# Eight-step rows for the first four chunks of k and b in a chunked recurrence with a feed-forward block, under a new written-out order

## The chip, the cores and the metric

The kernel runs on one core of a Trainium2 chip. The metric is device time in microseconds; several executions are timed and the median is given. A profile is one more execution, with the time of every instruction and DMA packet. Work is spread over five instruction queues: PE (matrix multiplies and transposes, results in PSUM), DVE and ACT (elementwise work, both can read PSUM), POOL (elementwise work, SBUF only) and SP (issues DMAs).

## The reference

`r, k, v, w, a, b` have the shape (4 batches, 8 heads, 768 steps, 40 features). For each of the 32 heads a 40 x 40 state is carried over the steps; the output of the recurrence goes through a feed-forward block with a squared ReLU:

```python
for t in range(S):
    y[:, :, t] = np.einsum('bhd,bhde->bhe', rt, state)
    Sa = np.einsum('bhde,bhe->bhd', state, at)
    state_decay = state * wt[:, :, None, :] - np.einsum('bhd,bhe->bhde', Sa, bt)
    state = state_decay + np.einsum('bhd,bhe->bhde', vt, kt)
...
h = x @ w_in            # x: (3072, 320), w_in: (320, 2048)
r = np.maximum(h, 0.0)
return (r * r) @ w_out  # w_out: (2048, 320)
```

## The kernel before

The 768 steps are cut into 12 chunks of 64. Inside a chunk the recurrence is written as matrix products; between chunks only the state is carried. The program is a list of named operations (`plan.add`, `ew`, `pe`), and a string `ORDER` (lines 87 to 214) says in which order they are issued and on which engine each one runs: `POOL castA 0` is the operation castA of chunk 0 on POOL; `PE2 TK 0` is the transposition TK of chunk 0, with its result in the second of four PSUM slots (`pb0` to `pb3`). Each engine takes its own operations strictly in that order and waits at the first whose inputs are not there or whose slot is not free. The order was not made at run time; it stands in the source.

What a chunk c does, by the names in `ORDER`:

- Loads on SP, two DMAs each (`load`, line 391): `ldw`, `ldk`, `ldb`, `ldv` in rows of 40 numbers (160 B, one step of one head), token-major, that is with the step on the partition; `lda`, `ldr` in rows of eight steps (1,280 B), with the head pair and the group of eight steps on the partition. Every raw buffer is there twice (`raw_kb` holds k and b of a chunk together). A DMA's semaphore is used again eight DMAs later, so SP issues a DMA only after the one eight before it has landed.
- Decay: `ln` (ACT) takes the logarithm of w into `lnW`; `hi` and `lo` split it into two bf16 parts; PE sums over the steps, once token-major in two halves (`ci h0`, `ci h1`) and once feature-major, with the step along the free axis (`cf`). ACT makes exponentials of these: `ex` (into `Gin`, for the output) and `ei` (with the sign reversed, into `iG`) from ci, `ef` (into `GT`) from cf.
- Keys: `mulKB h0`, `h1` multiply raw k and b by `iG` into `KB` (token-major, bf16); `TK` is 32 transposes of KB on PE, and `tK` copies them out of PSUM to `KBT` (feature-major). KB itself is an operand of `S` and `Y`, KBT of `EN`.
- a and r: `castA`, `castR` convert to bf16 in the order that the transposes want, `TA`, `TR` are 16 transposes each, `tA` multiplies by GT on the way out of PSUM, `tR` copies. Both go to `AR`.
- Recurrence: `EN` (KBT times a; `mEN` masks it), `AS` (a times the state, from chunk 1 on), `EV`, `u0`, `NU`, `u1` (solves for the chunk's right-hand sides in `VU`), `SC` and `S` (new state), `s` (decays it into `STb`), `TS` and `tS` (its transposition, `Sb`).
- Output: `TV`, `tV`, `CX`, `mCX`, `RS`, `Y`, `y`, `yd`, then `XT`, `xt` (x transposed).
- Feed-forward: for four blocks u, `F` (256 input features) and `FL` (the last 64), `f` (ReLU out of PSUM), `q` (square), `O`, then `o` and the store `st`.

The weights come in pieces: `lwl`, `lwi u0` to `u3` (staged in the second buffer of G) with casts `cwl`, `cwi`; `lwo x0` to `x7`, staged in the two `osb` buffers, with casts `cwo`. They share SP's queue with the loads of the chunks.

The lines the change and the prediction touch: 404 to 411 (loads of k and b), 475 to 478 (`ei`), 501 to 509 (`mulKB`), 522 to 534 (`TK`, `tK`), 547 to 556 (`steps`, `turned`, `tA`, which turn a transposed row-of-eight tile), 561 to 562 (what EN reads), and `ORDER`. In the profile all matmuls have line 384, all transposes 388, and copies 365 (DVE), 370 (ACT) and 374 (POOL).

Of the kernel before, what the change touches and what calls it, by code (L numbers as in the profile page):

```python
# [84 lines left out]
HALVES = ()  # L85
O_AFTER = 0
ORDER = """SP ldw 0; SP lda 0; SP ldb 0; SP ldk 0; ACT ln 0; SP ldw 1; POOL hi 0; POOL castA 0; DVE lo 0; PE0
TA 0; SP lda 1; PE1 ci 0 h0; PE2 ci 0 h1; ACT ex 0 h0 g1; PE3 cf 0; ACT ex 0 h1 g0; ACT ei 0 h1;
ACT ex 0 h1 g1; ACT ei 0 h0; SP ldv 0; ACT ef 0; DVE mulKB 0 h1; SP ldw 2; ACT ex 0 h0 g0; DVE
mulKB 0 h0; DVE tA 0 g0; PE2 TK 0; DVE tK 0; ACT ln 1; SP ldk 1; POOL hi 1; DVE tA 0 g1; PE3 EN 0  # L90
g0; POOL lo 1; DVE mEN 0 g0; PE1 EN 0 g1; DVE mEN 0 g1; SP ldb 1; PE2 ci 1 h1; POOL castV 0 g0;
ACT ei 1 h1; POOL castV 0 g1; ACT ex 1 h1 g1; ACT ex 1 h1 g0; POOL castA 1; PE0 EV 0; SP ldr 1;
PE3 cf 1; ACT u0 0; PE1 ci 1 h0; ACT ln 2; PE NU 0; ACT ex 1 h0 g1; PE2 TA 1; POOL hi 2; ACT ef 1;
SP lda 2; DVE lo 2; ACT u1 0 g0; DVE tA 1 g0; ACT ei 1 h0; SP ldv 1; PE3 S 0 g0; DVE tA 1 g1; ACT
ex 1 h0 g0; ACT u1 0 g1; PE1 ci 2 h0; SP ldr 0; ACT ex 2 h0 g1; PE S 0 g1; DVE mulKB 1 h0; PE2 TV
0; DVE mulKB 1 h1; ACT ei 2 h0; DVE s 0 q1; ACT tV 0; SP ldw 3; PE0 TK 1; DVE s 0 q0; SP ldk 2;
DVE tK 1; PE3 TS 0; ACT tS 0; PE2 EN 1 g1; PE0 cf 2; DVE mEN 1 g1; SP ldb 2; PE3 EN 1 g0; ACT ef
2; POOL castR 0; DVE mEN 1 g0; ACT ex 2 h0 g0; POOL castV 1 g1; ACT castA 2; PE2 TR 0; PE0 ci 2
h1; POOL castV 1 g0; ACT tR 0 g0; PE1 AS 1; SP lwl 0; ACT tR 0 g1; POOL castR 1; PE EV 1; ACT ln
3; PE3 CX 0 g0; PE2 CX 0 g1; ACT u0 1; POOL hi 3; DVE mCX 0 g0; ACT ex 2 h1 g1; PE NU 1; POOL lo  # L100
3; ACT ex 2 h1 g0; SP lwi 0 u0; ACT ei 2 h1; DVE mCX 0 g1; PE3 TR 1; ACT u1 1 g0; PE0 TA 2; ACT tR
1 g1; DVE tA 2 g1; PE2 Y 0; SP ldv 2; ACT tR 1 g0; ACT u1 1 g1; PE3 SC 1; DVE mulKB 2 h1; PE1 TV
1; SP ldr 2; PE S 1 g0; DVE tA 2 g0; ACT tV 1; PE S 1 g1; DVE y 0; DVE mulKB 2 h0; ACT cwl 0; DVE
yd 0; PE0 TK 2; DVE s 1 q0; PE1 ci 3 h1; POOL cwi 0 u0; SP lwi 0 u1; PE2 CX 1 g0; DVE tK 2; ACT ei
3 h1; ACT ex 3 h1 g0; ACT ex 3 h1 g1; SP lwo 0 x1; DVE s 1 q1; PE0 cf 3; PE1 EN 2 g0; DVE mCX 1
g0; ACT ef 3; PE3 TS 1; POOL castV 2 g1; SP lwo 0 x0; ACT tS 1; DVE mEN 2 g0; PE0 EN 2 g1; POOL
castR 2; PE2 AS 2; SP ldb 3; POOL castV 2 g0; DVE mEN 2 g1; PE3 ci 3 h0; PE1 XT 0; ACT ex 3 h0 g0;
POOL cwi 0 u1; ACT ei 3 h0; DVE xt 0; PE EV 2; ACT ex 3 h0 g1; SP lwi 0 u3; PE0 CX 1 g1; ACT u0 2;
PE1 FL 0 u1; DVE mCX 1 g1; PE NU 2; SP lda 3; PE3 RS 1; ACT u1 2 g0; PE0 SC 2; PE Y 1; DVE u1 2
g1; SP ldk 3; PE F 0 u1; DVE y 1; SP lwi 0 u2; DVE yd 1; PE S 2 g0; ACT f 0 u1; PE S 2 g1; PE2 TR  # L110
2; DVE s 2 q0; PE3 FL 0 u3; ACT tR 2 g1; POOL cwi 0 u3; DVE s 2 q1; ACT tR 2 g0; SP ldw 4; DVE q 0
u1; POOL castA 3; PE F 0 u3; POOL cwo 0 x0; PE1 TV 2; ACT f 0 u3; DVE cwo 0 x1; PE2 XT 1; PE0 TS
2; SP lwo 0 x2; ACT tV 2; PE3 F 0 u0; DVE tS 2; POOL mulKB 3 h0; DVE xt 1; PE0 TA 3; PE FL 0 u0;
SP lwo 0 x3; DVE tA 3 g1; PE2 FL 1 u3; ACT f 0 u0; PE1 CX 2 g0; POOL cwi 0 u2; DVE tA 3 g0; PE F 1
u3; SP ldv 3; DVE mulKB 3 h1; PE3 F 1 u2; ACT f 1 u3; DVE mCX 2 g0; SP ldr 3; PE0 TK 3; ACT ln 4;
PE FL 1 u2; PE2 FL 1 u1; DVE tK 3; PE1 CX 2 g1; ACT f 1 u2; POOL hi 4; PE F 1 u1; POOL cwo 0 x2;
DVE mCX 2 g1; PE3 F 1 u0; POOL lo 4; ACT cwo 0 x3; PE0 EN 3 g0; ACT f 1 u1; SP lwo 0 x5; PE FL 1
u0; DVE mEN 3 g0; PE1 F 0 u2; ACT f 1 u0; SP lwo 0 x4; PE FL 0 u2; DVE q 0 u0; PE2 EN 3 g1; POOL
castV 3 g0; PE0 cf 4; ACT f 0 u2; DVE mEN 3 g1; PE3 ci 4 h0; SP ldw 5; POOL castV 3 g1; ACT ef 4;
PE1 RS 2; DVE q 0 u2; PE Y 2; ACT ei 4 h0; PE2 AS 3; DVE yd 2; PE EV 3; DVE cwo 0 x5; ACT ex 4 h0  # L120
g1; DVE y 2; PE0 O 0 u0; SP lwo 0 x7; ACT u0 3; POOL cwo 0 x4; DVE q 1 u0; ACT ex 4 h0 g0; POOL
castR 3; ACT q 0 u3; PE1 ci 4 h1; SP lwo 0 x6; PE NU 3; ACT ex 4 h1 g1; PE3 TR 3; ACT u1 3 g0; SP
ldk 4; PE O 0 u1; DVE tR 3 g1; ACT ex 4 h1 g0; DVE u1 3 g1; ACT ei 4 h1; PE O 0 u2; POOL cwo 0 x7;
SP ldb 4; ACT tR 3 g0; ACT ln 5; PE1 XT 2; DVE cwo 0 x6; PE2 TV 3; SP lda 4; POOL hi 5; DVE xt 2;
PE3 SC 3; ACT tV 3; PE S 3 g0; POOL lo 5; PE S 3 g1; PE O 0 u3; DVE s 3 q1; SP ldv 4; DVE s 3 q0;
POOL q 1 u1; PE1 ci 5 h0; ACT o 0; PE2 CX 3 g0; SP ldk 5; PE3 cf 5; ACT ex 5 h0 g0; DVE mCX 3 g0;
PE0 FL 2 u1; ACT ef 5; PE F 2 u1; DVE mulKB 4 h0; ACT ex 5 h0 g1; PE2 F 2 u2; ACT f 2 u1; SP ldb
5; DVE mulKB 4 h1; POOL castA 4; PE3 FL 2 u3; PE FL 2 u2; ACT ei 5 h0; DVE q 2 u1; PE0 TK 4; ACT f
2 u2; PE1 TA 4; PE F 2 u3; DVE tA 4 g0; SP ldw 6; DVE tK 4; PE2 F 2 u0; POOL castV 4 g0; ACT f 2
u3; POOL castV 4 g1; PE FL 2 u0; DVE tA 4 g1; PE0 ci 5 h1; POOL q 2 u3; ACT f 2 u0; PE3 CX 3 g1;  # L130
PE1 O 1 u0; SP lda 5; DVE mCX 3 g1; ACT ex 5 h1 g1; ACT q 2 u0; PE2 EN 4 g1; PE3 EN 4 g0; POOL q 1
u2; DVE mEN 4 g1; PE O 1 u1; ACT ex 5 h1 g0; ACT ei 5 h1; SP st 0; DVE mEN 4 g0; PE0 RS 3; PE Y 3;
POOL mulKB 5 h0; SP ldr 4; PE2 AS 4; DVE y 3; PE EV 4; DVE q 1 u3; PE O 1 u2; SP ldw 7; DVE yd 3;
ACT ln 6; DVE mulKB 5 h1; PE O 1 u3; ACT u0 4; POOL hi 6; POOL q 2 u2; PE NU 4; ACT o 1; PE3 XT 3;
ACT u1 4 g0; PE0 TS 3; SP st 1; DVE xt 3; PE1 TK 5; ACT tS 3; DVE u1 4 g1; PE3 FL 3 u3; POOL castA
5; PE F 3 u3; SP ldv 5; DVE tK 5; POOL castR 4; PE2 TA 5; ACT f 3 u3; POOL lo 6; PE0 TV 4; SP lda
6; DVE tA 5 g1; PE1 O 2 u0; DVE tA 5 g0; DVE tV 4; ACT ln 7; PE3 SC 4; PE S 4 g0; SP ldb 6; PE S 4
g1; PE2 ci 6 h0; DVE s 4 q0; PE0 TR 4; ACT ex 6 h0 g0; PE O 2 u1; SP ldk 6; ACT ei 6 h0; DVE s 4
q1; ACT ex 6 h0 g1; DVE tR 4 g1; ACT tR 4 g0; PE3 cf 6; PE2 EN 5 g0; ACT ef 6; POOL castV 5 g1; PE
O 2 u2; DVE mEN 5 g0; SP ldr 5; POOL castV 5 g0; ACT q 3 u3; PE0 CX 4 g0; PE3 ci 6 h1; DVE mCX 4  # L140
g0; PE2 CX 4 g1; ACT ei 6 h1; POOL hi 7; PE O 2 u3; ACT castA 6; POOL lo 7; DVE mCX 4 g1; PE0 F 3
u0; ACT ex 6 h1 g0; ACT o 2; ACT ex 6 h1 g1; PE FL 3 u0; SP st 2; PE2 EN 5 g1; PE1 TA 6; ACT f 3
u0; DVE mEN 5 g1; PE3 RS 4; PE Y 4; SP ldw 8; ACT q 3 u0; PE0 AS 5; POOL mulKB 6 h1; DVE yd 4; PE
EV 5; DVE tA 6 g1; PE2 FL 3 u1; DVE y 4; SP ldv 7; ACT u0 5; PE F 3 u1; POOL mulKB 6 h0; DVE tA 6
g0; PE3 F 3 u2; SP ldv 6; ACT f 3 u1; PE FL 3 u2; POOL castR 5; PE1 XT 4; PE2 TK 6; ACT f 3 u2;
DVE xt 4; POOL q 3 u1; PE NU 5; DVE tK 6; SP ldr 6; PE1 TR 5; ACT u1 5 g0; PE3 F 4 u0; DVE tR 5
g1; ACT tR 5 g0; ACT u1 5 g1; PE FL 4 u0; PE2 EN 6 g1; PE1 EN 6 g0; ACT f 4 u0; DVE mEN 6 g1; PE0
SC 5; SP lda 7; PE S 5 g0; PE S 5 g1; ACT q 3 u2; PE3 ci 7 h0; DVE s 5 q1; PE2 O 3 u0; SP ldk 7;
ACT ei 7 h0; DVE mEN 6 g0; ACT ex 7 h0 g1; PE O 3 u1; ACT ex 7 h0 g0; SP st0 0; DVE s 5 q0; POOL
castV 6 g0; PE3 TV 5; PE1 ci 7 h1; DVE tV 5; POOL castR 6; PE0 TS 4; ACT ex 7 h1 g1; SP ldb 7; PE  # L150
O 3 u2; ACT ei 7 h1; POOL castA 7; DVE tS 4; ACT ex 7 h1 g0; ACT ln 8; SP ldr 7; PE3 CX 5 g0; PE1
# [66 lines left out]
def kernel(  # L218
# [128 lines left out]
    def evac(name, make, n, reads, writes, free):  # L347

        kind = " ".join(x for i, x in enumerate(name.split()) if i != 1)
        if kind not in HALVES:  # L350
            ew(name, make(slice(0, 2), 2 * n), reads=reads, writes=writes, free=free)
            return
# [607 lines left out]
```

## Time and profile before

| | |
|---|---|
| median of 3 runs | 252.59 us |
| the three runs | 251.22, 252.59, 256.84 us |
| span of the profiled execution | 249.1 us |
| PE, DVE, ACT, POOL busy | 219.2, 183.3, 172.4, 119.3 us |
| DMA packets | 115,179, of them 101,302 under 512 B |
| ACT `iG`<-pb (ei), 24 of them | 0.696 us each |
| ACT `GT`<-pb (ef), 12 | 1.022 us each |
| DVE `KB`<-raw_kb,iG (mulKB), 16; POOL, 8 | 0.992; 1.584 us each |
| DVE `KBT`<-pb (tK), 11 | 1.220 us each |
| DVE `AR`<-pb,GT (tA), 24 | 0.683 us each |
| DVE `Sb`<-pb (tS), 8; ACT, 3 | 0.820; 1.237 us each |
| POOL casts of raw a, r, v to bf16; ACT of raw a | 0.716 to 0.809; 0.736 us each |

The times hold no figure of their own for the profiled execution; the span, from its first to its last instruction, stands in its place. The table of groups gives, per line, engine, tiles and shape, the busy time and the mean of one instruction, so a step of the order is found by the tiles that it writes and reads. "Idle before" is the time that the engine stood still just before such an instruction, with what it waited for. A matmul's duration is that of one instruction from start to end; they overlap, so the distance from start to start is the price of one more.

### The profile page before, as it was taken

How to read it: one execution, taken by the hardware profiler on the slowest of the kernel's cores; microseconds unless marked ns; L12 is line 12 of the kernel's file. 1: busy time of each engine (PE TensorE's matmuls, PEld its weight loads, DVE VectorE, ACT ScalarE, POOL GpSimd, SP SyncE). 2: the span in 40 equal slices, each digit the busy share in tenths (PEclk: the TensorE clock that was granted, in tenths of full speed). 3: DMA queues.
4: the chain of work that ended last, by engine and by line, in shares of the span. 5: the costliest groups of instructions: out<-in, count | busy, mean ns of one | idle time of the engine just before them, and what ended most of it. 6: DMA issues, size and time to landing. Idle time of an engine off the chain costs nothing.

```text
span 249.1 us, 12580 instructions
## 1 busy us (share of the span) xinstructions
PE 219.2 (88%) x5752; PEld 171.4 (69%) x5752; DVE 183.3 (74%) x227; ACT 172.4 (69%) x231; POOL 119.3 (48%) x119
## 2 busy tenths in 40 slices
PE   0458868859997999999999999999999999999991
...
DMA  6999899989998986978868978965580020201121
GB/s 130 168 157 212 158 190 182 229 195 218 224 195 161 157 199 122 189 159 147 184 171 136 179 121 217 157 163 115 119 144 4 4 58 4 56 3 30 26 52 55
DMA packets 115179, 33.58 MB, mean 135 GB/s; under 512 B 101302, under 2 KB 115126, under 8 KB 115126
## 3 DMA queue, kind: packets, MB, share of 16 engines
q1 hardware_dynamic: 114982, 32.62, 65.3%
q8 instruction: 45, 0.74, 1.2%
...
## 4 chain that ended last, share of the span: by engine, by line
PE 51%; SPq 21%; DMA 8%; DVE 6%; ACT 6%; issue 4%; POOL 3%; POOLq 0%; ACTq 0%
PE pb L384 45%; SPq L407 8%; PE pb L388 5%; SPq L431 3%; SPq L421 3%; SPq L400 2%; SPq L882 2%; SPq L414 2%; DMA osb<-in_moe_w_out_dram 2%; DMA G<-in_moe_w_in_dram 2%; DMA raw_w<-in_w_dram 2%; DMA raw_r<-in_r_dram 2%; DVE AR L365 1%; ACT AR L370 1%; DMA out_dram<-osb 1%
## 5 line engine op out<-in xcount | busy, mean ns | idle before, releaser
L384 PE MATMUL pb<-WOUT,G 128*128 128x320 bf16 x384 | 57.2, 300 | 1.1 <-DVE WOUT L365 1.1
L802 ACT ACTIVATE G<-pb 128x1024 bf16<-128x1024 f32 x44 | 44.6, 1021 | 19.3 <-PE pb L384 18.4
L810 POOL TENSOR_TENSOR G<-G 128x1024 bf16<-128x1024 bf16 x21 | 40.8, 1956 | 24.2 <-ACT G L802 24.1
L384 PE MATMUL pb<-XT,WIN 128*128 128x256 bf16 x384 | 48.4, 273 | 2.8 <-POOL WIN L374 2.8
L384 PEld LDWEIGHTS <-G 128*128 128x128 bf16 x384 | 35.3, 98 | 15.8 <-issue 2.3
L384 PEld LDWEIGHTS <-WIN 128*128 128x128 bf16 x384 | 34.9, 98 | 10.4 <-POOL WIN L374 3.3
L578 DVE TENSOR_TENSOR CX<-pb,MSKI 128x1024 bf16<-128x1024 f32 x24 | 29.0, 1220 | 7.4 <-PE pb L384 7.3
L578 DVE TENSOR_TENSOR EN<-pb,MSK 128x1024 bf16<-128x1024 f32 x24 | 29.0, 1221 | 6.5 <-PE pb L384 6.2
L481 ACT ACTIVATE Gin<-pb 64x320 f32<-64x320 f32 x48 | 20.6, 429 | 9.8 <-PE pb L384 9.2
L374 POOL CAST VU<-raw_v 64x640 bf16<-64x640 f32 x24 | 18.7, 777 | 11.8 <-DMA raw_v<-in_v_dram 11.1
L370 ACT ACTIVATE osb<-pb 128x640 f32<-128x640 f32 (+1 forms) x13 | 8.3, 640 | 18.6 <-PE pb L384 18.1
L670 DVE TENSOR_TENSOR STb<-pb,GT 64x640 bf16<-64x640 f32 x22 | 18.0, 820 | 2.9 <-PE pb L384 2.6
L374 POOL CAST hi<-lnW 128x640 bf16<-128x640 f32 x12 | 9.0, 747 | 22.7 <-ACT lnW L453 19.4
L380 DVE TENSOR_TENSOR KB<-raw_kb,iG 128x640 bf16<-128x640 f32 x16 | 15.6, 992 | 5.7 <-DMA raw_kb<-in_b_dram 3.2
L384 PEld LDWEIGHTS <-EN 64*64 64x64 bf16 x768 | 15.3, 114 | 5.9 <-issue 2.7
L475 ACT ACTIVATE iG<-pb 128x640 f32<-128x640 f32 x24 | 16.7, 696 | 3.4 <-PE pb L384 3.2
L553 DVE TENSOR_TENSOR AR<-pb,GT 128x512 bf16<-128x512 bf16 x24 | 15.8, 683 | 2.3 <-PE pb L388 2.0
L384 PE MATMUL pb<-XT,WLAST 64*128 64x256 bf16 x192 | 17.4, 274 | 0.1
L808 DVE TENSOR_TENSOR G<-G 128x1024 bf16<-128x1024 bf16 x13 | 10.4, 805 | 8.6 <-ACT G L802 8.5
L370 ACT ACTIVATE VUT<-pb 128x2048 bf16<-128x2048 bf16 x8 | 15.0, 1874 | 2.2 <-PE pb L388 2.2
L370 ACT ACTIVATE VU<-pb 64x640 bf16<-64x640 f32 x19 | 13.2, 696 | 3.7 <-PE pb L384 3.5
L378 POOL TENSOR_TENSOR KB<-raw_kb,iG 128x640 bf16<-128x640 f32 x8 | 12.6, 1584 | 6.2 <-ACT iG L475 4.5
...
## 6 DMA issues: line engine op xcount, KB each, us to landing
...
```

The lines of the kernel that those rows point to most:

```text
L370: alts.append(("ACT", c_act(n), lambda: nc.scalar.activation(out=o_(), in_=i_(), func=ACTF.Copy, scale=1.0 if scale is None else scale)))
L374: lambda: nc.gpsimd.tensor_copy(out=o_(), in_=i_())))
L380: ("DVE", c_dve(n), lambda: nc.vector.tensor_tensor(out=o_(), in0=a_(), in1=b_(), op=op))]
L384: return lambda: nc.tensor.matmul(out=o_(), lhsT=l_(), rhs=r_(), start=start, stop=stop, skip_group_check=True)
L407: nc.sync.dma_start(out=raw_kb[c % NKBR][rows(g if nm == "b" else 1 - g), NJ * g:NJ * g + NJ, :], in_=half(x, g))
L475: ew(f"ei {c} h{jh}", [("ACT", c_act(2 * n), lambda hb=hb, jh=jh: nc.scalar.activation(out=iG[0][:].rearrange("p (g j) e -> p g (j e)", g= ...
L481: nc.scalar.activation(out=Gin[c % NGI][rows(g), NP * jh:NP * jh + NP, :].rearrange("p j e -> p (j e)"), in_=slot(hb, FP32)[rows(g), g, 0: ...
L553: ew(f"tA {c} g{g}", [("DVE", c_dve(512), lambda g=g: nc.vector.tensor_tensor(out=steps(AR[q2][:, 0, g]), in0=turned(ha, g), in1=steps(GT[ ...
L578: evac(f"m{nm} {c} g{g}", lambda s, n: [("DVE", c_dve(n), lambda: nc.vector.tensor_tensor(out=dst[q2][:, g, s].rearrange("p q i t -> p (q ...
L670: ew(f"s {c} q{q}", [("DVE", c_dve(2 * n), lambda q=q: nc.vector.tensor_tensor(out=STb[q2][rows(q), :, q, 0:D], in0=slot(hs, FP32)[rows(q) ...
L802: ("ACT", c_act(1024), lambda gb=gb, hf=hf: nc.scalar.activation(out=gb, in_=slot(hf, FP32)[:], func=ACTF.Relu)),
L810: ("POOL", 1900, lambda gv=gv: nc.gpsimd.tensor_tensor(out=gv, in0=gv, in1=gv, op=ALU.mult)),
```

## The change

For the chunks in `BY8 = (0, 1, 2, 3)`, k and b are loaded as a and r are, in rows of eight steps, `raw_kb` holding k in its first 16 head places and b in the other 16. They are converted to bf16 (`castk`, `castb`, on POOL or ACT), transposed (`Tk`, `Tb`, 16 transposes each) and multiplied by the reversed-sign exponential of the feature-major sums (`eg`, from cf, in place of the two `ei`) on the way out of PSUM into KBT (`tk`, `tb`, two halves each, on DVE). The token-major KB is then made from KBT by a second transposition (`TU`, 32 transposes) and a copy (`tU`, DVE or ACT). Chunks 4 to 11 go on as before (`keys`). EN reads KBT by halves. The order is another one from the first entry to the last: 1,052 entries instead of 1,032. Entries of the planner's past in the source (`LAT`, `HALVES`, `evac` and so on) are gone; they issued nothing of their own.

```diff
+BY8 = (0, 1, 2, 3)
...
         for nm, x in (("k", k), ("b", b)):
             def go(nm=nm, x=x):
+                if c in BY8:
+                    xv = x[:, :, t0, :].rearrange("b (p q) (k i) e -> q (b p) k (i e)", q=2, i=8)
+                    to = raw_kb[c % NKBR][:].rearrange("p (x q j) e -> p x q (j e)", x=2, q=2)
+                    for q in range(2):
+                        nc.sync.dma_start(out=to[:, int(nm == "b"), q, :], in_=xv[q])
+                    return
...
+    def keys_by8(c, hf):
+        q2 = c % 2
+        igt = iG[0][:].rearrange("p h e -> p (h e)")[:, 0:1024].rearrange(
+            "p (m t) -> p m t", t=L)
+        ew(f"eg {c}", [("ACT", c_act(1024), lambda: nc.scalar.activation(
+            out=igt.rearrange("p (g m) t -> p g m t", g=2),
+            in_=slot(hf, FP32)[:].rearrange("p g (m t) -> p g m t", t=L), func=ACTF.Exp,
+            scale=-1.0))],
+           reads=[hf], writes=[("iG", 0), ("iG", 1)], free=[hf])
+        kb = KB[c % NK]
+        for x, nm in enumerate("kb"):
+            ew(f"cast{nm} {c}", copy_alts(
+                lambda x=x: kb[:, 16 * x:16 * x + 16, 0:D].rearrange(
+                    "p (i q) e -> p q i e", q=2),
+                lambda x=x: raw_kb[c % NKBR][:, 16 * x:16 * x + 16, :].rearrange(
+                    "p (q i) e -> p q i e", q=2), 640, engines=("POOL", "ACT")),
+               reads=[("raw", nm, c % NKBR)], writes=[("KB", c % NK, x)])
+            h = ("A", "T" + nm, c)
...
+            pe(f"T{nm} {c}", "R", 64, ms, reads=[("KB", c % NK, x)], writes=[h], alloc=[h])
+            for g in range(2):
+                ew(f"t{nm} {c} g{g}", [("DVE", c_dve(512), lambda g=g, x=x, h=h:
+                                        nc.vector.tensor_tensor(
+                    out=steps(KBT[q2][:, NP * g:NP * g + NP, g if x else 1 - g]),
+                    in0=turned(h, g), in1=steps(igt[:, NP * g:NP * g + NP]), op=ALU.mult))],
+                   reads=[h, ("iG", 0), ("iG", 1)], writes=[("KBT", q2, x, g)], free=[h])
...
+        pe(f"TU {c}", "R", 64, ms, reads=KX, writes=[h2], alloc=[h2])
+        ew(f"tU {c}", copy_alts(
+            lambda: kb[:].rearrange("p (i q) e -> p q i e", q=2)[:, :, :, 0:D],
+            lambda: slot(h2, BF16)[:].rearrange("p q (i e) -> p q i e", e=64)[:, :, :, 0:D],
+            1280, True),
+           reads=[h2], writes=[("KB", c % NK, 0), ("KB", c % NK, 1)], free=[h2])
...
+            if c not in BY8:
...
+        if c in BY8:
+            keys_by8(c, hf)
+        else:
+            keys(c)
```

The new order around chunk 2, cut to a few entries:

```
PE1 AS 1; ...; ACT ef 2; ACT ex 2 h1 g1; ACT ex 2 h1 g0; PE3 TA 2; ...; PE2 Tk 2; ACT eg 2;
DVE tA 2 g0; PE0 ci 2 h0; ACT castR 1; ACT castb 2; DVE tA 2 g1; ...; PE EV 1; PE3 Tb 2; ...; ACT u0 1
```

On SP the weights' pieces `lwo x6`, `lwo x7` now stand ahead of `lda 4`, `ldk 4`, `ldb 4`, `ldw 6`, `ldv 4`; in the order before `lwo x7`, `lwo x6` stood ahead of `ldk 4`, `ldb 4`, `lda 4`, `ldv 4`.

More of the change, by code (lines that the diff above doesn't have):

```diff
@@ L82, in issue @@
         assert len(done) == len(self.ops)
[L85 to L151, printed above, removed]
@@ new lines @@
+h0; PE1 O 0 u0; PE NU 3; PE O 0 u1; POOL q 1 u1; PE2 XT 2; DVE q 0 u2; ACT ex 4 h1 g0; PE0 TR 3;
+DVE xt 2; ACT u1 3 g0; SP lda 4; ACT u1 3 g1; PE3 TV 3; SP ldk 4; PE2 SC 3; PE S 3 g0; DVE tR 3 g1;
+ACT tR 3 g0; POOL q 0 u3; SP ldb 4; POOL q 1 u0; ACT tV 3; PE S 3 g1; POOL castA 4; DVE s 3 q0; PE
+O 0 u2; PE3 CX 3 g0; DVE s 3 q1; POOL q 1 u2; POOL mulKB 4 h1; PE0 CX 3 g1; DVE mCX 3 g0; PE2 FL 2
+u1; PE F 2 u1; ACT cwo 0 x6; DVE mCX 3 g1; PE3 F 2 u2; ACT cwo 0 x7; PE O 0 u3; PE0 F 2 u0; PE FL 2
@@ new lines @@
+u0; ACT ln 5; SP ldw 6; SP ldv 4; ACT f 2 u1; DVE o 0; PE FL 2 u2; ACT f 2 u2; PE2 FL 2 u3; DVE hi
+5; POOL castV 4 g0; PE1 TA 4; PE F 2 u3; SP ldr 4; DVE lo 5; PE3 O 1 u0; ACT f 2 u0; PE O 1 u1; ACT
+f 2 u3; SP ldb 5; ACT q 2 u3; DVE tA 4 g0; DVE mulKB 4 h0; DVE tA 4 g1; POOL q 2 u1; PE2 ci 5 h0;
+SP ldk 5; ACT ei 5 h0; ACT ex 5 h0 g1; SP lda 5; PE1 TK 4; PE0 cf 5; POOL castR 4; PE O 1 u2; ACT
+ef 5; PE0 ci 5 h1; DVE q 1 u3; POOL q 2 u2; SP st 0; DVE tK 4; SP lda 6; PE1 EN 4 g0; SP ldk 6;
+POOL mulKB 5 h0; DVE mEN 4 g0; SP ldv 5; ACT ex 5 h0 g0; ACT ln 6; ACT ex 5 h1 g1; ACT castV 4 g1;
@@ new lines @@
+g0; DVE s 6 q1; PE0 EN 7 g1; DVE s 6 q0; ACT ei 8 h1; POOL q 4 u2; DVE mEN 7 g1; ACT ex 8 h1 g1;
+PE1 cf 8; PE2 RS 6; ACT f 5 u0; ACT ef 8; PE Y 6; PE3 AS 7; PE EV 7; SP lda 9; PE1 TR 8; DVE y 6;
+PE0 TA 8; DVE yd 6; ACT u0 7; SP ldk 9; ACT tR 8 g0; DVE tR 8 g1; SP ldr 10; POOL castR 7; DVE tA 8
+g1; DVE tA 8 g0; PE2 ci 8 h0; SP ldb 8; POOL castV 8 g0; PE NU 7; ACT q 5 u1; ACT ei 8 h0; PE1 O 4
+u0; ACT ex 8 h0 g1; PE O 4 u1; ACT ex 8 h0 g0; PE O 4 u2; DVE mulKB 8 h1; ACT ln 9; POOL hi 9; POOL
+castA 9; SP st 3; POOL q 5 u0; DVE u1 7 g0; PE O 4 u3; ACT u1 7 g1; DVE mulKB 8 h0; POOL castV 8
```

300 lines of the change are left out of this document (176 added, 124 removed).

## The prediction, made before the changed kernel had run

> **What bounds the kernel now.** First the page: the span and the engines in forty slices.
>
> ```profile
> span 249.1 us, 12580 instructions
> PE 219.2 (88%) x5752; PEld 171.4 (69%) x5752; DVE 183.3 (74%) x227; ACT 172.4 (69%) x231; POOL 119.3 (48%) x119
> ...
> PE   0458868859997999999999999999999999999991
> ...
> DMA  6999899989998986978868978965580020201121
> ```
>
> No engine is full overall, but PE is from slice 10 (62 us) on, and DMA is full before it. The busy table over stretches that I cut at the chunk recurrence puts figures on this (PE, PEld, DVE, ACT, POOL busy, clock, DMA share, GB/s):
>
> ```profile
> 10.00:30.00 20.00, 14.00 (x400) 11.29 (x396) 13.91 (x16) 14.62 (x23) 6.32 (x9) 1.00 1.02 180
> 30.00:60.00 30.00, 22.80 (x770) 18.40 (x766) 22.65 (x28) 21.86 (x32) 11.74 (x13) 0.89 0.92 198
> 60.00:76.40 16.40, 15.99 (x414) 12.36 (x414) 12.37 (x16) 14.45 (x21) 9.12 (x11) 1.00 0.92 204
> 76.40:244.00 167.60, 164.47 (x4154) 127.92 (x4150) 126.57 (x146) 118.25 (x154) 88.20 (x71) 1.00 0.56 113
> ```
>
> From 76.4 us PE is 98% busy, so loads are worth something before that only. Third, PE's timeline, for the dates: `STb,AR` is AS, the state going into chunks 1, 2 and 3; `VU,EN` is EV; the first `XT,WIN` lines are F 0; `VU,KB` at 76.35 is S 3.
>
> ```profile
> 31.37 0.48 PE L384 MATMUL pb<-STb,AR 128*64 128x80 bf16 x16
> 31.78 0.68 PE L384 MATMUL pb<-VU,EN 64*64 64x40 bf16 x32
> ...
> 44.54 0.48 PE L384 MATMUL pb<-STb,AR 128*64 128x80 bf16 x16
> ...
> 50.98 1.05 PE L384 MATMUL pb<-XT,WIN 128*128 128x256 bf16 x8
> ...
> 56.04 1.05 PE L384 MATMUL pb<-XT,WIN 128*128 128x256 bf16 x8 [2.84 <-POOL WIN L374]
> ...
> 69.15 0.48 PE L384 MATMUL pb<-STb,AR 128*64 128x80 bf16 x16
> ...
> 76.35 0.66 PE L384 MATMUL pb<-VU,KB 128*64 128x40 bf16 x32
> ```
>
> The 2.84 us is the one long wait of PE that a late weight load causes. I compare three stages: to AS 2 (44.54), to S 3 (76.35), to PE's end (244.0).
>
> **Loads.** Eight (k and b of chunks 0 to 3) go from 2,048 rows of 160 B to 256 rows of 1,280 B. The price of the second kind, from a window that holds one 320 KB store in such rows:
>
> ```profile
> q1 hardware_dynamic: 288, 0.33, 13.7%
> ```
>
> 13.7% of 10 us = 1.37 us. The whole run: 65.3% of 249.1 = 162.7 us; its 13,824 larger packets at 1.37/256 take 74.0; the other 88.7 us over 48 loads are 1.85 each. Gain 8 x 0.48 = 3.8 us. The trace's packet records (means of 16.0 and 75.7 ns, over 16 engines) give 2.05 and 1.21, and SP needs two issues of some 0.65 us for a load, so 1.3: 8 x 0.75 = 6.0 us. Ends 3.8 and 6.0; I take 6.0, since mixed loads are what the records hold. Up to the last WOUT piece 18 loads in short rows at 2.05, 8 in long rows at 1.3 and weights of 19.1 (2,560 packets at 58.7 ns, 2,048 at 75.7) make 66.4 us; now 10 and 16: 60.4. [...]
>
> **Work of chunks 0 to 3.** ACT: eight `iG` exponentials at 0.70 (5.6) become four at 1.02 (the GT row) with five casts at 0.74 and two tU at 1.24 (the Sb row): 10.3, +4.7. DVE: seven mulKB at 0.99 and four tK at 1.22 (11.8) become sixteen multiplies out of PSUM at 0.683 (AR<-pb,GT, the same shapes; 0.82, the STb row, as upper end) and two tU at 0.82: 12.6, +0.8 (to +3.0). POOL: one mulKB (1.58) becomes three casts (2.25). PE: 128 more 64x64 transposes; sixteen take 0.61 us at 21.77 us and 0.41 at 30.34, that is 27 and 15 ns each: 1.9 to 3.4. All this stands in the stretch where PE, DVE and ACT are 70 to 76% busy: room is there, but not on the chain.
>
> **Stage 1, to AS 2.** I follow the new order by hand with these durations. In before's timeline a load lands 7.2 to 9.2 us after the sum of the loads up to and with it (raw_r of chunk 2: 37.8, landed 44.95; the last WIN piece: 50.9, landed 60.06); I use 7.5, and 9 for weights. Chunk 0: cf 0 ends 9.7, eg 10.8, ef 11.9; DVE tb, tA, tk to 15.9; mEN 0 to 18.3, tU 0 19.2, EV 0 19.4 (before: 19.3), s 0 done 25.7 (before 26.9). EN of chunk 0 no longer waits for the token-major form. Then two waits are new. v 1 stands at 23.3 us of loads, as before, so EV 1 cannot be early. And EV 1 now stands in PE's queue behind ci 2 h0, whose slot eg 2 must free: on ACT ef 2 ends 31.5, two exponentials 32.5, eg 2 33.5, so EV 1 comes at 34.0, 2.2 later than 31.78, and on ACT u0 1 behind castR 1 and castb 2 at 35.7; behind these wait NU, u1, S of chunk 1. What follows is quicker, since k 2, b 2 and v 2 are long there (v 2 stood at 36.5 us of loads, now at 30): u1 38.7, S 1 40.5; DVE, after mEN 2 g1, ends s 1 at 42.9; AS 2 at 43.1. Stage 1: -1.4. SP's wait for castb 0 (raw_kb is reused by ldb 2, ahead of ldk 1 and lda 1) is hidden by four loads in flight; uncovered, 0.74.
>
> **Stage 2, to S 3.** F 0 u1 comes at 52.5 (50.98 before) since S 2 and XT 1 now precede it. WIN is complete at 54.4 (44.3 us of loads, 9, and the cast of 1.04) instead of 60.5, so the 2.84 us wait goes. From F 0 u1 to EV 3 before: 18.6 us less 2.84 = 15.7 for 13.5 us of matmuls at full pace (15 ns a small one, 109 and 136 ns those of 256 and 320 columns, from the x16 rows of the late timeline); after 13.7, so 16 us: EV 3 at 68.5. From there 6.0 us of matmuls took 6.8 before; the new order has 4.4, so 5: S 3 at 73.5. What is late next is ACT and DVE (each some 24 us of work from AS 2 to S 3, before and after) and POOL: WOUT stages through two `osb`, and lwo x6, x7 wait for POOL's cwo x4, x5 behind a 1.96 us square; loads of chunk 4 queue behind them on SP and start near 69 (72.4 before). S 3: -2.9, of it stage 2 -1.5.
>
> **Stage 3, to the end.** Matmuls at full pace: 152.8 against 151.8 us from S 3 on. Where neighbouring groups differ in tile shape, the trace shows 0.10 to 0.13 us lost (F to FL at 154.09: 0.97 for 8 x 0.109); the new order has 123 such places, the old 136: -1.3. DVE gets 6 us more of work here on 127 of 167.6, which PE hides; uncovered places could cost 0 to 6. Stage 3: -0.3.
>
> Sum: -1.4 - 1.5 - 0.3 = -3.2, span 245.9. The times given hold no time for the profiled execution itself; its span lies 2.1 below the fastest run (251.22) and 3.5 below the median, 252.59. With 3.5: **249.4 us**.
>
> **Rivals.** *The load relief reaches S 3 whole*: the 6.0 us come through, if PE, ACT and DVE close up behind the loads. For it: DMA share 1.02 and 0.92 until 76 us. Against it: EV 1 and F 0 come no earlier in the stages above. Span 249.1 - 6.0 - 0.3, time 246.3.
>
> *Full line rate*: rows of eight pass at the best slice of the traffic (373 GB/s in a 20 to 40 us window), 0.88 us a load, 8 x 0.97 = 7.8 and a time of 244.5. SP's 1.3 us a load speaks against it. [...]
>
> *ACT and DVE take the place of the loads* (the slower one): the added 4.7 us of ACT and 0.8 us of DVE in chunks 0 to 3 fall on the chain (eg before EV 1, castb before u0, tU before EV), one behind the other, and the earlier loads only wait. Span 249.1 + 5.5 - 0.3, time 257.8. It decides if AS 2 comes after 47 us. For it: ACT is 73% busy from 10 to 60 us, and EV 1 is late by the walk too; against it: before, DVE and POOL stand waiting for loads there.
>
> *A cold PE*: the three groups of 32 transposes at 25.2 to 28.0 took 1.03 us each and the next groups 0.61, so nearly 3 us of them did not raise the pace (the granted clock reads 1.00 there). If the 15 ns pace comes at F 0 (52.5) instead of 30, some 600 small matmuls cost 12 ns more, 7 us, half of it in idle time: 249.4 + 3.6 = 253.0. [...]
>
> **How the numbers follow.** Three runs before spread from 251.22 to 256.84, so about 2% (5 us) is what can be told from no change. Forecast, within 2%: 0.41 (own range 247 to 253). Whole relief 0.27 and line rate 0.03: faster by over 2% (below 247.5), 0.30. ACT and DVE 0.23: slower. Cold PE 0.06: within, 0.04, with ACT's delay slower, 0.02. So within 2% 0.45, slower 0.25. The range goes from just below the whole relief, 245.0, to 257.8; outside lie the line rate, 0.03, some of the whole relief, 0.05, and half of the slower case, 0.12.
>
> **What would show it.** Packets fall by 8 x 1,792 = 14,336, from 115,179 to about 100,800. AS 1 to AS 2 on PE's timeline: EV 1 near 34, AS 2 near 43. PE's wait for WIN gone; F 0 from 52.5; S 3 near 73.5. From there to PE's end 167 us. AS 2 before 41 and S 3 before 71 would make the whole relief right; AS 2 after 47 the added work of ACT and DVE; 0.61 us for sixteen transposes after 35 us the cold PE. PE waits of over 3 us in the sum after 76 us would say that stage 3 was mis-sized.

## The result, and the profile after

| | before | after |
|---|---|---|
| median | 253.19 us of 4 runs beside it (251.22 to 256.84) | 260.69 us of 4 runs (259.17 to 261.85) |
| ratio | | 1.0297, 95% interval 1.0218 to 1.0375 |
| span of the profiled execution | 249.1 us | 257.2 us |

The change costs 3% where 249.4 us, within 2% of no change, was forecast, and the time lies above the range. Some executions of a kernel come out longer than its others, so the ratios leave those out while the medians hold them, and the profiles of the first moved PE order, of "before, then after", of "second PE order, then before" and of the last early order are of such executions. The page of the changed kernel, where the prediction had the span, the engines and the DMA queue (a line of section 3 is queue, kind, packets, MB, share of 16 engines):

```profile
span 257.2 us, 12861 instructions
PE 223.3 (87%) x5880; PEld 177.2 (69%) x5880; DVE 190.9 (74%) x239; ACT 174.2 (68%) x232; POOL 125.1 (49%) x118
...
DMA packets 100844, 33.60 MB, mean 131 GB/s; under 512 B 84918, under 2 KB 100790, under 8 KB 100790
...
q1 hardware_dynamic: 100646, 32.62, 59.2%
q8 instruction: 46, 0.75, 1.3%
```

The loads did what they were to do: 14,335 packets fewer, q1 at 59.2% for 65.3. Two of the stretches, with the prediction's columns:

```profile
30.00:60.00 30.00, 23.68 (x786) 19.46 (x781) 21.66 (x28) 21.45 (x31) 10.09 (x11) 0.83 0.91 219
...
76.40:252.00 175.60, 165.46 (x4191) 130.21 (x4183) 130.85 (x151) 121.33 (x158) 86.06 (x67) 1.00 0.53 106
```

At 76.4 us next to nothing is lost: S 3 comes at 77.07 for 76.35. The last stretch has become 8 us longer, and in it PE is busy for only 1 us more: 10.1 us idle for 3.1. PE's timeline (start, us, line, tiles, shape, count, idle time before and what ended it) gives the dates that the prediction named (`STb,AR` is AS 2, `VU,EN` EV 1, `XT,WIN` F 0 u1, `VU,KB` S 3):

```profile
33.06 0.68 PE L364 MATMUL pb<-VU,EN 64*64 64x40 bf16 x32
...
43.41 0.74 PE L364 MATMUL pb<-STb,AR 128*64 128x80 bf16 x16 [0.21 <-DVE STb L714]
...
56.92 1.92 PE L364 MATMUL pb<-XT,WIN 128*128 128x256 bf16 x16
...
77.07 0.66 PE L364 MATMUL pb<-VU,KB 128*64 128x40 bf16 x32
```

What PE waits for (line, what it waited for, us in the sum, times, longest):

```profile
PE pb L368 <- issue: 7.2, 6, 2.2
PE pb L368 <- ACT iG L542: 1.9, 1, 1.9
PE pb L364 <- issue: 1.8, 3, 1.1
```

"Issue" is time in which an engine waits for nothing that the profile shows. Neither this view nor PE's timeline of the kernel before has such a wait of PE. Here there are nine, 8.9 us (9.0 in the expectations, from the two rounded sums), and on the timeline every one stands where no wait should be, in the middle of a run of equal matmuls:

```profile
38.39 0.18 PE L364 MATMUL pb<-VU,KB 128*64 128x40 bf16 x1 [1.07 <-issue]
47.22 0.36 PE L368 MATMUL pb<-IDb,tR 64*128 64x64 bf16 x13 [0.74 <-issue]
52.59 0.21 PE L368 MATMUL pb<-IDb,VU 64*128 64x64 bf16 x1 [2.06 <-issue]
97.77 0.44 PE L368 MATMUL pb<-IDb,STb 64*128 64x64 bf16 x18 [1.14 <-issue]
101.77 0.20 PE L368 MATMUL pb<-IDb,VU 64*128 64x64 bf16 x2 [0.22 <-issue]
135.49 0.45 PE L368 MATMUL pb<-IDb,KB 64*128 64x64 bf16 x19 [0.84 <-issue]
149.15 0.33 PE L368 MATMUL pb<-IDb,tA 64*128 64x64 bf16 x11 [2.16 <-issue]
168.89 3.28 PE L364 MATMUL pb<-WOUT,G 128*128 128x320 bf16 x23 [0.39 <-issue]
210.64 0.62 PE L364 MATMUL pb<-KB,CX 128*64 128x40 bf16 x27 [0.30 <-issue]
```

A group of 16 or 32 that ends in x13 or x1 after a wait has been cut. Counting PE's matmuls from the first one, the cuts stand after number 731, 987, 1115, 2138, 2266, 3161, 3545, 4057 and 5081: the distances are multiples of 128, to within one. 128 matmuls with their weight loads are 256 instructions. q8, the instruction queue, moved 46 packets (0.75 MB, 16 KB each), and PE's 5,880 matmuls and 5,880 weight loads are 45.9 times 256; in the kernel before it moved 45, and 11,504 such instructions are 44.9 times 256.

Theory 1: PE's instructions come in blocks of 256, and a block needs some 4 us to follow the one before (an estimate: the two blocks with a wait at either end took 4.00 us, from 97.77 to 101.77, and 5.37, from 47.22 to 52.59); where an order runs 128 small matmuls (15 ns each, 1.9 us) without wide ones between, PE stands still at the block's edge. What a block takes by itself, the run with 1,024 transposes below shows.

The trace's packet records show the wait itself. Each of the nine ends 1.2 to 1.5 us after a packet of the instruction queue q8 has landed; four of them:

| wait of PE ends at, us | 52.59 | 97.77 | 149.15 | 210.64 |
|---|---|---|---|---|
| last q8 packet before it | 50.06 to 51.11 | 95.17 to 96.32 | 146.52 to 147.77 | 208.27 to 209.26 |

In the fifteen kernels profiled for this case that have such waits there are 99 of them, and every one ends 1.2 to 1.9 us after such a packet. So these are waits for instructions.

To size it, I split the time from S 3 to PE's last group by the distances from each matmul's start to the next:

| us, S 3 to the last group | before | after |
|---|---|---|
| whole | 166.8 | 175.1 |
| inside groups | 127.7 | 135.0 |
| from one group to the next (waits, changes of shape) | 39.1 | 40.1 |

The gaps at the six cuts behind S 3 hold 6.3 us from start to start. That is the growth inside the groups but for 1.0, since the new order has one group O more to do behind S 3.

Rivals: 2, the extra work of the by-eight keys; 3, operands and buffers of the new order; 4, the loads' traffic; 5, the granted clock gives back what is won.

### The profile page after: what moved, and what is told of

The parts are those of the page before. It is cut to its first block, busy times and chain, and to the rows that moved or that the text cites. A ratio compares the mean times of both kernels' runs of the same rounds, so it can differ in the third digit from the quotient of the medians.

```text
span 257.2 us, 12861 instructions
## 1 busy us (share of the span) xinstructions
PE 223.3 (87%) x5880; PEld 177.2 (69%) x5880; DVE 190.9 (74%) x239; ACT 174.2 (68%) x232; POOL 125.1 (49%) x118
## 2 busy tenths in 40 slices
DMA packets 100844, 33.60 MB, mean 131 GB/s; under 512 B 84918, under 2 KB 100790, under 8 KB 100790
## 3 DMA queue, kind: packets, MB, share of 16 engines
q1 hardware_dynamic: 100646, 32.62, 59.2%
## 4 chain that ended last, share of the span: by engine, by line
PE 68%; DVE 10%; ACT 10%; issue 7%; DMA 2%; POOL 1%; SPq 0%; DVEq 0%; ACTq 0%; POOLq 0%
PE pb L364 59%; PE pb L368 9%; DMA raw_w<-in_w_dram 2%; DVE EN L622 2%; ACT VUT L350 1%; DVE G L852 1%; ACT Gin L548 1%; DVE lo L360 1%; DVE AR L345 1%; DVE hi L345 1%; DVE AR L597 1%; ACT iG L471 1%; ACT GT L564 1%; ACT KBT L350 1%; DVE STb L714 1%
## 5 line engine op out<-in xcount | busy, mean ns | idle before, releaser
L854 POOL TENSOR_TENSOR G<-G 128x1024 bf16<-128x1024 bf16 x26 | 50.5, 1956 | 38.3 <-ACT G L846 33.3
L846 ACT ACTIVATE G<-pb 128x1024 bf16<-128x1024 f32 x39 | 39.4, 1021 | 22.4 <-PE pb L364 21.9
L364 PE MATMUL pb<-XT,WIN 128*128 128x256 bf16 x384 | 47.3, 273 | 0.0
L358 POOL TENSOR_TENSOR KB<-raw_kb,iG 128x640 bf16<-128x640 f32 x9 | 14.1, 1570 | 11.3 <-ACT iG L542 9.0
L358 POOL TENSOR_TENSOR lo<-lnW,hi 128x640 bf16<-128x640 f32 x9 | 12.6, 1399 | 11.8 <-DVE hi L345 11.8
L354 POOL CAST VU<-raw_v 64x640 bf16<-64x640 f32 x18 | 12.9, 715 | 9.8 <-DMA raw_v<-in_v_dram 9.1
L364 PE MATMUL pb<-UTI,hi 64*128 64x64 bf16 x192 | 9.1, 206 | 7.8 <-POOL hi L354 7.7
L354 POOL CAST hi<-lnW 128x640 bf16<-128x640 f32 x7 | 5.7, 812 | 20.4 <-ACT lnW L519 10.8
L784 DVE TENSOR_TENSOR Yb<-pb,Gin 128x128 bf16<-128x128 f32 (+1 forms) x24 | 12.5, 550 | 4.2 <-PE pb L364 4.1
L364 PEld LDWEIGHTS <-hi 64*128 64x128 bf16 x192 | 7.7, 105 | 10.5 <-POOL hi L354 7.7
```

The lines of the kernel that those rows point to most:

```text
L354: lambda: nc.gpsimd.tensor_copy(out=o_(), in_=i_())))
L358: return [("POOL", 40 + 2.35 * n, lambda: nc.gpsimd.tensor_tensor(out=o_(), in0=a_(), in1=b_(), op=op)), ("DVE", c_dve(n), lambda: nc.vect ...
L364: return lambda: nc.tensor.matmul(out=o_(), lhsT=l_(), rhs=r_(), start=start, stop=stop, skip_group_check=True)
L784: return [("DVE", c_dve(2 * (f1 - f0)), lambda: nc.vector.tensor_tensor(out=Yb[q2][:, :, to:to + f1 - f0], in0=slot(hy, FP32)[:, :, f0:f1] ...
L846: ("ACT", c_act(1024), lambda gb=gb, hf=hf: nc.scalar.activation(out=gb, in_=slot(hf, FP32)[:], func=ACTF.Relu)),
L854: ("POOL", 1900, lambda gv=gv: nc.gpsimd.tensor_tensor(out=gv, in0=gv, in1=gv, op=ALU.mult)),
```

## The experiments

The median of the kernel before was 252.09 us on one chip and 255.19 on another, so each ratio goes by runs of the kernel before on the same chip.

**The same orders, blocks cut elsewhere.** PE has nothing to do for its first 7.7 us; small transposes of a constant are put there, 76 in the kernel before, 16 and 48 in the changed one:

```diff
     with tc.manual_schedule():
+        pad = ps.tile([128, 2, 1024], BF16, name="pb3", tag="pb3", bufs=1)
+        for i in range(76):
+            tp(lambda: pad[:, i % 2, 0:64], lambda: UTI[rows(i % 2), :], i % 2)()
         plan.issue(ORDER)
```

> The kernel before, its order and all its work untouched, with 76 transpositions of a constant put in front of TensorE's first group, where TensorE waits for its first operand anyway; they move every later block boundary (256 TensorE instructions are 128 matmuls with their weight loads) 76 matmuls forward in the program. Theory 1 (a block of TensorE instructions cannot follow the one before it in less than about 4 us, and where the order runs 128 small matmuls in less, TensorE stands still in the middle of a group): in the trace of the kernel before, the blocks cut at the new places would be short of 4.0 us by 10.1 us in the sum, against 3.5 us at the places where they are now, so the time rises by 4 to 7 us, to 257 to 260, and the waits view shows TensorE waiting for 'issue', 4 us or more, at matmul counts that stand one whole number of blocks apart. Rival 2 (those waits come from the eight-step keys, from their reads or their traffic): the kernel before has none of these, so no such wait and a time of 253 +- 1. Rival 3 (a matter of the order alone, of buffers and operands): the order is that of before, so 253 +- 1.

> The changed kernel with 16 transpositions of a constant ahead of TensorE's first group, nothing else touched. Theory 1: with its stalls taken out, its trace cut at the places 16 matmuls earlier in the program is short of 4.0 us by 7.8 us, against 11.0 us at the present places, so 1 to 3 us faster than the changed kernel (258 to 260), with the 'issue' waits at other groups than before. Rivals 2 and 3: the same waits at the same groups, 260.7 +- 1.

> The changed kernel with 48 transpositions of a constant ahead of TensorE's first group, nothing else touched. Theory 1: cut 48 matmuls earlier its trace is short of 4.0 us by 14.8 us, against 11.0, so 2 to 4 us slower than the changed kernel (262.5 to 264.5), with more 'issue' waits (12 us or more). Rivals 2 and 3: 260.7 +- 1.

| | median, us | ratio to before | "issue" waits of PE |
|---|---|---|---|
| before with 76 | 256.53 | 1.0144 (1.0098 to 1.0191) | 3.9 us, 7 times |
| after with 16 | 261.56 | 1.0197 (1.0077 to 1.0317) | 11.7 us |
| after with 48 | 262.60 (before 253.49) | none | 8.9 us |

The kernel before, without a single by-eight key, gets the waits. Two of the seven on its timeline:

```profile
49.76 0.56 PE L384 MATMUL pb<-AR,VUT 64*128 64x64 bf16 x14 [0.73 <-issue]
...
155.76 0.37 PE L384 MATMUL pb<-VU,KB 128*64 128x40 bf16 x13 [1.50 <-issue]
```

In all three kernels the cuts fall at counts of 89 to 94 over a multiple of 128, the padding included, and so as many matmuls earlier in the order: with 16, TV 2 and TV 4 are cut after 15 and 14 of their 32 transposes, where it had been 31 and 30; all other cuts fall in other groups. That is against rivals 2 and 3. The sizes I had wrong: the first rose by 3.6 us (0.0144 x 253) where 4 to 7 stood, and the two others cannot be told from the changed kernel, where a gain and a loss were expected. The sum of shortfalls over blocks was not a measure of the time lost; why, no run shows. Not all of the first kernel's loss is shown to be waits, either: its profile has 1.7 us more behind S 3 (168.5 for 166.8), and S 3 itself 2.8 us later at a granted clock of 0.66 from 30 to 60 us (0.89 before). The clock does not explain the ratio, since over the runs that it rests on it is the same, 0.970 and 0.971.

**The rate by itself.** In the kernel before, 1,024 such transposes ahead of everything, and 1,024 behind (one execution).

> The kernel before with 1,024 small transpositions of a constant (64x64, operands always there, no wait) ahead of TensorE's first group and 1,024 more behind its last; this measures how fast TensorE's instructions come by themselves, with and without the kernel's own loads running. Theory 1 (blocks of 256 instructions that follow each other no faster than about 4 us): both stretches show 128 matmuls in about 4 us, with a gap of about 2 us in each block, so some 8 x 4 = 32 us for each stretch. Rivals 2 and 3 (no such limit): 128 matmuls in 1.9 us at the 14.5 ns that such groups take in the profile after 30 us (3.4 us at the 27 ns that they take before 30 us), evenly, so 15 us for the last stretch and at most 27 for the first.

The timeline at the end, when no loads run, and then at the start, with them:

```profile
279.77 2.04 PE L388 MATMUL pb<-IDb,UTI 64*128 64x64 bf16 x128 [1.12 <-issue]
283.52 2.04 PE L388 MATMUL pb<-IDb,UTI 64*128 64x64 bf16 x128 [1.70 <-issue]
287.26 2.04 PE L388 MATMUL pb<-IDb,UTI 64*128 64x64 bf16 x128 [1.70 <-issue]
290.72 2.04 PE L388 MATMUL pb<-IDb,UTI 64*128 64x64 bf16 x128 [1.42 <-issue]
```

```profile
9.48 2.04 PE L388 MATMUL pb<-IDb,UTI 64*128 64x64 bf16 x128 [0.92 <-issue]
13.48 2.80 PE L388 MATMUL pb<-IDb,UTI 64*128 64x64 bf16 x128 [1.96 <-issue]
18.30 3.38 PE L388 MATMUL pb<-IDb,UTI 64*128 64x64 bf16 x128 [2.03 <-issue]
23.13 2.04 PE L388 MATMUL pb<-IDb,UTI 64*128 64x64 bf16 x128 [1.44 <-issue]
```

x128, then a wait, again and again, with no operand to wait for. From start to start a block takes 3.46 to 3.75 us at the end, and 4.0 to 4.8 here (5.1 for a later one) under the loads. That is 27 to 29 ns for a small matmul at best, for 15 when its instruction is there. In this run it is the loads that make the difference and not the clock: at the same granted clock of 0.60, the block from 27.13 took 5.10 us with the DMA engines 66% busy, and the one from 32.23 took 3.46 with them 2% busy. The packet records show what a block waits for. In the stretch at the end, the packet of the next block starts 1.0 to 1.6 us after a block has begun, takes 0.9 to 1.3, and the next block begins 1.2 to 1.6 us after it has landed. So there each block was fetched only once the one before it ran. The kernel before, cut at count 92, has one block under 4.0 us between S 3 and 195 us (3.59 at 95.5). In the changed kernel the blocks before the cuts at 97.8 and 149.1 would, without the gap, have taken 2.3 and 2.4.

**The loads alone.** The changed kernel with k and b of the four chunks again in runs of 160 B:

```diff
-                    xv = x[:, :, t0, :].rearrange("b (p q) (k i) e -> q (b p) k (i e)", q=2, i=8)
-                    to = raw_kb[c % NKBR][:].rearrange("p (x q j) e -> p x q (j e)", x=2, q=2)
+                    xv = x[:, :, t0, :].rearrange("b (p q) (k i) e -> q (b p) k i e", q=2, i=8)
+                    to = raw_kb[c % NKBR][:].rearrange("p (x j q) e -> p x q j e", x=2, q=2)
```

> The changed kernel with one part undone: k and b of the first four chunks arrive in 160-byte runs again (16 times as many packets for these loads less none elsewhere, 14,336 more in the sum), but in the same by-eight layout but for the place of the step in the row, and with the same work and order. What the loads are worth by themselves: by theory 1 the loads are a small gain, 1 to 2.5 us slower than the changed kernel (EV 1 and AS 2 some 1.5 us later), the 'issue' waits stay at about 9 us. Rival 4 (the traffic of the loads was the bound of the first 45 us): 4 us or more slower. If the loads were hidden throughout: 260.7 +- 1.

263.87 us, 1.0532 of before (1.0466 to 1.0597), against 1.0297 for the changed kernel; 115,180 packets. AS 2 comes 1.5 us later than in the changed kernel (44.9) and S 3 1.7 later (78.8): the -1.4 that the forecast gave the loads. That much was expected; the whole was not (1 to 2.5 us expected, 3.2 by the medians and more by the ratios). The remaining 3 us come after S 3, all inside groups (138.6 for 135.0 us), where chunks 4 to 11 load as before. Of these, 1.1 stand at the cuts (7.4 for 6.3). For the rest there are two stretches of 3.4 us, from 153.7 and from 211.7, at a granted clock of 0.50, where the changed kernel has 1.00: an estimate of up to 1.7 us each. "Issue" waits of 9.0 us are there as well. As the cause of the 3% rival 4 has the sign against it: the loads are a gain.

**PE's order alone.** 87, then 90 of PE's 398 groups of the changed kernel moved (some into other PSUM slots), the other engines untouched; a piece of the second:

```diff
 PE NU 5
 PE F 3 u1
+PE2 TS 4
 PE3 F 4 u0
+PE0 SC 5
 PE FL 4 u0
-PE0 TS 4
-PE1 TV 5
+PE2 TV 5
+PE1 O 3 u0
+PE3 TR 5
 PE2 TK 6
```

> The changed kernel with all its work, its loads and the orders of ACT, DVE, POOL and the loads untouched; only TensorE's own order is changed: 87 of its 398 groups are moved, so that the wide groups of the feed-forward part stand between the runs of small matmuls. Theory 1: the 9.0 us of 'issue' waits fall to 3 or less and the time to 250 to 254. Rival 2 (the extra DVE, ACT and TensorE work of the eight-step keys is what costs): 260 +- 1.5, since all of it is still there. Rival 3 (TensorE waits for operands and buffers in the new order): no forecast of a gain, as no operand comes earlier; 258 to 262.

> A second order of TensorE's groups alone for the changed kernel (90 of 398 groups moved, ACT, DVE, POOL and loads in their order), since the first left TensorE's waits between groups longer by 8 us. In this one, counted on the replay of the changed kernel's own durations, no wait between groups grows. Theory 1 (the 9.0 us of 'issue' waits are the loss): 'issue' waits of 4 us or less, stage 3 (S 3 to TensorE's end) at 168 to 171 instead of 175, time 253 to 257. Rival 2 (the extra work of the eight-step keys): 260 +- 1.5. Rival 5 (the granted clock falls as soon as TensorE stands still less, so that nothing is won): 'issue' waits down, granted clock down from 0.98 to 0.95 or less, 259 to 263.

The first: 263.17 us, 1.0271 (1.0161 to 1.0381); the second: 257.67 us, 1.0255 (1.0129 to 1.0381). The waits of PE for "issue" in the first, which fell from 8.9 us to 3.3:

```profile
PE pb L367 <- issue: 2.4, 2, 2.0
...
PE pb L363 <- issue: 0.9, 2, 0.6
```

Forecast missed in both. In the second the "issue" waits are 5.3 us (4 or less expected), and S 3 to the last group takes 174.0 (168 to 171 expected). The time inside groups behind S 3 does fall from 135.0 to 130.7, but from group to group it rises from 40.1 to 43.3: groups moved for the sake of the blocks now stand in front of operands that are not ready. Half of this speaks for theory 1, the other half for rival 3, and the ratio does not decide.

**Whole new orders.** All engines and the loads reordered, for both kernels.

> The changed kernel's work and loads in another order on every engine, with the runs of small matmuls broken by wide ones: what the by-eight loading is worth where TensorE's instructions come in time. Theory 1: 'issue' waits of 4 us or less and 247 to 254. Rival 2: 257 or more. Rival 5: granted clock 0.95 or less and 255 to 260.

> The kernel before (160-byte loads, keys scaled token-major, no second transposition) with its groups in another order, found in the same manner as that of the last run; the two differ by the data path alone, each in an order of its own. If the by-eight path is a gain in itself (theory 1 with the 1.5 us of the first 45 us): this one is 1 to 3 us slower than the last. If its extra work costs more than its loads give (rival 2): 3 us or more faster. In itself 245 to 252.

268.36 us, 1.0635 (1.0537 to 1.0734), and 264.12 us, 1.0474 (1.039 to 1.0558): both far slower than where they started. The first waits 8.0 us for POOL's KB; the second has AS 2 at 48.2. By the expectation recorded with them, a gain of 3 us or more of the second over the first speaks for rival 2, and the second is faster by 4.2. But the two orders differ throughout, and these runs do not tell that from the difference of the data paths.

**Two proven orders, joined at S 3.** Neither kernel's order is invented here: up to S 3 the one, from there what is left in the sequence of the other (in the third run the joint lies some 20 us behind S 3). The joint in the changed kernel:

```diff
 PE S 3 g0; DVE tR 3 g1; ACT tR 3 g0; POOL q 0 u3;
-SP ldb 4; POOL q 1 u0; ACT tV 3; PE S 3 g1; POOL castA 4; ...
+DVE q 1 u0; PE O 0 u2; POOL cwo 0 x7; ...
```

> The changed kernel, its by-eight loads and its order on every engine up to S 3 g0, and from there on the kernel before's order of what is left (TensorE's last 294 of 398 groups stand exactly as in the kernel before, and since the by-eight keys add 128 matmuls in the sum, the blocks of 256 instructions are cut at the same places of this part, too). Theory 1: no 'issue' wait of TensorE after S 3; from S 3 to TensorE's last group 167 to 168 us as in the kernel before (166.8), not 175.1; so S 3 at 77, span 249 to 250.5, time 251 to 254. Rival 2 (the extra work of the by-eight keys): that lies ahead of S 3 for the most part, so no forecast for the last part; 256 or more if what it delays is what runs late. Rival 5 (the granted clock gives back what the waits lose): 172 us or more from S 3 on at a clock of 0.95 or less.

> The reverse: the kernel before, without any by-eight load or key, in its own order until after S 3, and from there on in the changed kernel's order. Theory 1: the waits for 'issue' come back in a kernel that has no by-eight work at all: 4 to 8 us of them after S 3, and from S 3 to TensorE's last group 172 to 175 us; time 257 to 261. Rival 2 and the DMA rivals: no by-eight keys, no change in loads, so 253 +- 1.5.

> The candidate for the best: the first part of the second TensorE order (S 3 at 74.3 in its run), and some 20 us behind S 3 the kernel before's order of what is left. Theory 1: S 3 at 74 to 75, then 167 to 169 us: span 246.5 to 249, time 249 to 252, that is 0.99 to 1.00 of the kernel before, and so about the 1.4 + 1.5 us that the loads and the shorter second stage were forecast to give. If it is 254 or more, something besides the waits for instructions is lost in the by-eight part.

| | median, us | ratio to before | S 3 to last group, us |
|---|---|---|---|
| after, then before | 251.85 | 1.0014 (0.9973 to 1.0056) | 168.4 |
| before, then after | 261.24 | 1.0304 (1.0225 to 1.0383) | 177.1 |
| second PE order, then before | 251.85 | 0.9992 (0.9943 to 1.0040) | 168.8 |

That settles in which part of the program the time is lost, and that the by-eight work is not the cause. With the last part of the old order the changed kernel, all its by-eight work in place, takes the time of the kernel before; with the last part of the new order the kernel before, which has no such work, is as slow as the changed one (1.0304 for 1.0297). Their "issue" waits on PE's timeline, of the first kernel all of them, of the second those from S 3 (78.6) to 155:

```profile
40.15 0.36 PE L367 MATMUL pb<-IDb,KBT 64*128 64x64 bf16 x13 [0.23 <-issue]
44.97 0.36 PE L367 MATMUL pb<-IDb,tR 64*128 64x64 bf16 x13 [0.46 <-issue]
50.35 0.19 PE L367 MATMUL pb<-IDb,VU 64*128 64x64 bf16 x1 [2.06 <-issue]
```

```profile
99.82 0.40 PE L386 MATMUL pb<-IDb,STb 64*128 64x64 bf16 x15 [1.53 <-issue]
115.27 0.24 PE L382 MATMUL pb<-KB,CX 128*64 128x40 bf16 x3 [0.16 <-issue]
123.55 0.56 PE L382 MATMUL pb<-VU,KB 128*64 128x40 bf16 x23 [0.31 <-issue]
139.45 0.41 PE L386 MATMUL pb<-IDb,KB 64*128 64x64 bf16 x16 [1.28 <-issue]
144.00 0.35 PE L382 MATMUL pb<-AR,VUT 64*128 64x64 bf16 x12 [0.30 <-issue]
152.83 0.29 PE L386 MATMUL pb<-IDb,tA 64*128 64x64 bf16 x8 [1.41 <-issue]
```

The first has none behind S 3; the second has 6.1 us at its cuts there. The second is cut in the same groups as the changed kernel, TS 3 (STb), TK 7 (KB) and TA 8 (tA), three matmuls later in each, and in three more. Ahead of S 3 it has three further waits, 2.8 us, though its program up to there is that of the kernel before, which has none: whether a cut costs time also depends on the execution. The third run's time lies in its forecast (249 to 252 us), but not by the way that was forecast: in its profile S 3 comes at 79.1, not at 74 to 75, behind two waits for instructions of 3.1 and 2.9 us. Rival 5 falls here too: 168.4 us and a granted clock of 0.99 from 76.4 us on.

**The early part.** Open was why S 3 came at 77.1 and not at 73.5. Only early groups of "after, then before" were moved: 21 of PE's, then 33 of PE's with some of ACT's, DVE's and POOL's.

> after_then_before with 21 of TensorE's early groups moved, nothing else. Theory 1 for the early part: its 2.7 us of 'issue' waits before S 3 fall to about 1, S 3 g0 at 74 to 75 instead of 76.5, the rest as there (168): 249.5 to 251.5, 0.99 of the kernel before. If operands and buffers are late: S 3 at 76 to 77, 252 +- 1. If it is the granted clock between 30 and 60 us: S 3 at 76 to 77 with few 'issue' waits and a clock of 0.85 or less there.

> after_then_before with 33 early groups of TensorE, some 30 each of ACT's and DVE's early instructions and 15 more to POOL moved; loads and the last part as there. If operands and buffers are what is late in the early part: S 3 at 72 to 74, 247 to 250, 0.98 to 0.99 of the kernel before. Theory 1 alone: no more than the run before, 249.5 to 251.5. If the moves delay what the last part needs: 254 or more.

254.27 us, 1.0008 (0.9934 to 1.0083), S 3 at 77.0; and 256.22 us, 1.0034 (0.9996 to 1.0073), S 3 at 78.7. Neither helped, and neither tells the causes apart. In the first the "issue" waits ahead of S 3 did not fall from 2.7 us but rose to 3.9, of which 3.3 is one wait that ends at 39.8, 7.0 us after the edge before. The granted clock does not explain S 3 either: from 30 to 60 us it rose from 0.72 to 0.82. So what is lost between AS 2 and S 3 is in part waits for instructions, and the rest stays open. No version tried here is faster than the kernel before.

## Why the prediction was wrong

Right: the packets (100,844); stage 1 (AS 2 at 43.41 for 43.1, EV 1 at 33.06 for 34.0), which the run with short rows confirms; PE's wait for WIN is gone. That AS 2 came so close is partly luck: u1 was done at 37.3 for 38.7, and S 1 then stood for 1.07 us at a cut (38.39), which the walk did not have. Wrong as rivals: ACT and DVE in place of the loads (AS 2 came before 47), the whole relief (S 3 came after 71) and, with it, the full line rate. The sign of the cold PE does appear, sixteen transposes in 0.61 us at 38.51, but they take 0.41 again at 59.06; the granted clock from 30 to 60 us was 0.83 for 0.89, and what that cost was not measured by itself. The upper end, 257.8, had the right sign for a reason that did not occur.

Stage 2, S 3 at 73.5: it came at 77.07. F 0 u1 came at 56.92 for 52.5, and of those 4.4 us 2.8 are the waits for "issue" that end at 47.22 and 52.59 (0.74 + 2.06). How the rest divides is not settled, nor is the lateness of S 3 as a whole.

Of the 11.3 us between forecast and result, 8.6 stand in stage 3 and 3.6 ahead of S 3, less 0.9 behind PE's last group.

The step that failed is stage 3, "Matmuls at full pace: 152.8 against 151.8 us from S 3 on", then "-0.3". It measured +8.3 (175.1 for 166.8). The 1.0 of matmuls came, as the one group O more. What the step lacked is the 6.3 us at the cuts, where PE waits for the next 256 instructions: the pace of single groups was taken for the pace of a sequence, and I did not ask how fast the sequence's instructions come. With the old order put back in this part it took 168.4, that is 0.5 above before once the same group O is counted. The smaller terms: the -1.3 for changes of shape did not show (from group to group +1.0, with one new wait of 1.9 us on ACT's iG); DVE's 6 us, which I had as the danger, cost nothing that I can see, its busy time rising by 4.3 in the stretch. "PE waits of over 3 us in the sum after 76 us" was the test for this step, and it said so.

The hint stood in the source: the class Plan of the kernel before still holds `LINE, FETCH = 256, 4350`, and I had passed it over as a leftover of a planner. No code uses it; that it means 256 instructions and 4,350 ns is my reading. The runs show the 256; for the time, the 1,024 transposes show 3.46 to 5.1 us a block.
